# Two cached attention blocks on one core: three of the sixteen output-weight loads as sixteen transfers of 8 partitions each

## The chip, the cores and the metric

The kernel runs on one core of a Trainium2 chip. A core has five engines that run side by side: TensorE (PE; its weight loads are listed apart as PEld), VectorE (DVE), ScalarE (ACT), GpSimd (POOL) and SyncE (SP). Each has its own list of instructions and waits for the others by semaphores. Data comes from device memory into SBUF, which has 128 partitions, by DMA: an instruction on an engine's queue hands a transfer to the core's 16 DMA engines, which raise a semaphore when their share has landed. The metric is the time of one execution on the device in microseconds (us), lower being better.

## The reference, cut to what matters

Two independent blocks, A and B, with the same shapes; each is a decode step of attention over a key and value cache, followed by an output projection.

```python
def block(x, k_cache, v_cache, wq, wo):      # x [8, 1, 1024]; caches [8, 32, 4096, 128]; wq [1024, 4096]; wo [4096, 1024]
    q = (x @ wq).reshape(8, 1, 32, 128).transpose(0, 2, 1, 3)
    scores = jnp.einsum("bhqd,bhkd->bhqk", q, k_cache) * (128 ** -0.5)
    p = softmax(scores, axis=-1)
    o = jnp.einsum("bhqk,bhkd->bhqd", p, v_cache)
    return o.transpose(0, 2, 1, 3).reshape(8, 1, 4096) @ wo
out = concatenate([block(A), block(B)], axis=-1)
```

Everything is bfloat16. The four caches hold 256 MB each, and each is read once.

## The kernel before

**Steps.** The work is cut into 128 steps. A step is one batch row and one group of four heads: `gi` (0 to 15) counts cache and head group, and eight batch rows make up a group. One step needs 4 MB of keys and 4 MB of values. In SBUF a 4 MB load is 128 partitions by 32 KB: partition `h * 32 + p` holds 128 consecutive positions of head `h`.

**The loop.** Line 381 runs over `n`. In round `n` the keys of step `n` are loaded (`load_k`, line 217), multiplied by the query on DVE in two halves (`multiply`, line 263), summed over the head dimension by PE with the identity matrix (`add_up`, line 275) and by DVE (`reduce`, line 283). Step `m = n - 1` goes through its softmax on DVE and ACT, its values are loaded (`load_v`, line 224) and PE multiplies them with the probabilities (`pv`, line 321). Two rounds behind, PE and DVE gather the heads' outputs (`gather`, `heads`). Three rounds behind, after the last batch row of a group, `project` (line 347) multiplies the group's outputs with that group's 512 rows of the output weights and adds to the accumulator `acc`.

**Buffers and queues.** Keys and values have two buffers each (`NB = 2`), and so have the output weights (`wob`, one MB a buffer, chosen by `gi % 2`). Loads of keys, values and weights are all issued on SP's queue, in the order of the program: in round `n` first the keys of `n`, then, once in eight rounds (`m % 8 == 4`), the output weights of the group, then the values of `m`. SP holds an issue back until the buffer is free: a key load waits for DVE's last multiplication on that buffer, a value load for PE's `pv`. The two `x` loads and three of the four output stores are issued on ACT's queue; the last store is on SP's. These six transfers have 8 partitions each.

**The output-weight load.** `load_wo` (line 235) is one DMA per group. Its source is 512 rows of `wo`, its target 128 partitions by four pieces of 2 KB. It marks the buffer's name `wo0` or `wo1` as written, and `project` reads that name. The names are the planner's: `P.add` and `dma` record which operation reads and writes which name, `finish` turns that into semaphore waits in front of an instruction, and each DMA name has a semaphore of its own that counts to 16 per transfer. The weights of group `gi` are issued in the fifth round of the group and used five rounds later; for the first group that is 93.1 us and 231.3 us.

Of the kernel before, what the change touches and what calls it, by code (L numbers as in the profile page):

```python
# [94 lines left out]
def _build(nc, caches, out):  # L95
    x0, k0, v0, wq0, wo0 = caches[0]
    B, Sq, D = x0.shape
# [15 lines left out]
    assert Sq == 1 and Dh == 128 and Sk == 4096 and D == 1024 and H % HP == 0 and B == 8  # L113
    assert RS * H * Dh == T * Dh and R == NB * RS
    scale = float(Dh) ** -0.5

    es = ExitStack()
    with es:
        block = es.enter_context(nc.Block())

        def sb(name, shape, dt):
            return es.enter_context(nc.sbuf_tensor(name, shape, dt))

        def ps(name, shape):
            return es.enter_context(nc.psum_tensor(name, shape, FP32))
# [10 lines left out]
        wob = sb("wob", [128, 2, HP, D], BF16)  # L136
# [10 lines left out]
        on = sb("on", [128, 2, HP, B], BF16)  # L147
# [4 lines left out]
        acc = ps("acc", [128, 512])  # L152
# [4 lines left out]
        P = Program()  # L157

        def dma(eng, dst, src, writes, sem, reads=()):
            return P.add(eng, lambda e: e.dma_start(dst, src), reads=reads, writes=writes, dma=sem)  # L160
# [26 lines left out]
        def load_wq(which, c, s):  # L187
            i = slot(which)
            w = bufs[which][:, i, :].rearrange("p (r n) -> p r n", r=RS)
            src = caches[c][3].rearrange("(p r) n -> p r n", r=R)[:, s * RS:(s + 1) * RS, :]  # L190
            dma("sp", w, src, [f"{which}{i}"], f"{which}{i}")
            return f"{which}{i}", w
# [42 lines left out]
        def load_wo(gi):  # L235
            c, g = divmod(gi, NG)
            i = gi % 2
            src = caches[c][4][g * HP * Dh:(g + 1) * HP * Dh, :].rearrange("(h p) n -> p h n", p=Dh)
            dma("sp", wob[:, i], src, [f"wo{i}"], f"wo{i}")

        def make_qbc(n):
            gi, b0 = divmod(n, B)
# [104 lines left out]
        def project(gi):  # L347
            c, g = divmod(gi, NG)
            i = gi % 2

            def emit(e):
                last = None
                for hh in range(HP):
                    for half in range(2):
                        last = e.matmul(acc[32 * half:32 * half + B, :], on[:, i, hh, :], wob[:, i, hh, half * 512:(half + 1) * 512],  # L355
                                        start=(g == 0 and hh == 0), stop=(g == NG - 1 and hh == HP - 1),
                                        tile_position=(0, 32 * half))
                return last
            P.add("pe", emit, reads=[f"on{i}b{b}" for b in range(B)] + [f"wo{i}"], banks=["acc"])
            if g == NG - 1:  # L360
                for half, eng in ((0, "dve"), (1, "act")):
                    dst, src = orow[32 * half:32 * half + B, c, :], acc[32 * half:32 * half + B, :]
                    if eng == "dve":
                        P.add(eng, lambda e, dst=dst, src=src: e.tensor_copy(dst, src), writes=[f"orow{c}{half}"], banks=["acc"])
                    else:
                        P.add(eng, lambda e, dst=dst, src=src: e.activation(dst, src, ACTF.Copy), writes=[f"orow{c}{half}"], banks=["acc"])
                for half in (1, 0):
                    q = "sp" if c == NC - 1 and half == 0 else "act"
                    dma(q, out[:, 0, c * D + half * 512:c * D + (half + 1) * 512], orow[32 * half:32 * half + B, c, :],
                        [f"out{c}{half}"], "out", reads=[f"orow{c}{half}"])  # L370

        NS = NC * NG * B
        kslot, vslot = {}, {}
        first = [(s,) + load_wq("v", 0, s) for s in range(R // RS)]
        for c in range(NC):
            make_xT(c)
# [4 lines left out]
        for n in range(NS + 3):  # L381
# [3 lines left out]
            if 0 <= m < NS:  # L385
                last = m == NS - 1
                if m % B == 4 and m // B < NC * NG - 1:
                    load_wo(m // B)
                load_v(m, 4 if last else 1)
                if last:  # L390
                    load_wo(m // B)
# [12 lines left out]
            if n - 3 >= 0 and (n - 3) % B == B - 1:  # L404
                project((n - 3) // B)
# [58 lines left out]
def bass_concat_heads__mha_block_cached__mha_block_cached__decode_kernel(  # L464
    nc, A_x, A_k_cache, A_v_cache, A_wq, A_wo, B_x, B_k_cache, B_v_cache, B_wq, B_wo, out,
):
    caches = [(A_x, A_k_cache, A_v_cache, A_wq, A_wo), (B_x, B_k_cache, B_v_cache, B_wq, B_wo)]
    _build(nc, caches, out)
# [28 lines left out]
```

## Time and profile before

| what | value |
|---|---|
| median of 3 runs | 2599.2 us (2596.18 to 2600.48) |
| the profiled execution's own time | 2599.03 us |
| its span (first to last instruction) | 2597.2 us |
| around the span (own time less span) | 1.8 us |
| bytes read from device memory | 1107.33 MB, 426 GB/s over the span |
| PE busy | 1589.6 us (61%) |
| DVE busy | 1421.9 us (55%) |
| ACT busy | 391.0 us (15%) |
| output-weight loads | 16, 1024 KB each, 30.8 us from issue to landing |
| `project` on PE (line 355) | 128 matmuls, 16.6 us busy |

The profile is of one execution. "Busy" is the time in which an engine executed instructions, and engines overlap, so shares don't add up to one. For DMA the page has the mean busy share of the 16 DMA engines in 40 slices of the span, the packets of each queue, and the median time from the issue of a transfer to its landing; that time includes the wait behind transfers that were issued earlier. The chain of work that ended last is followed back from the last instruction, at each step to whatever released it. Besides the page, the trace holds a record for each DMA packet (start, duration, bytes, queue) and for each increment of a DMA semaphore.

### The profile page before, as it was taken

The numbers are of one execution on the slowest core, as the hardware profiler recorded it, in microseconds if no ns is written. First come the engines' busy times: TensorE is split into PE (matmuls) and PEld (weight loads), VectorE is DVE, ScalarE is ACT, GpSimd is POOL, SyncE is SP. The second block draws the span as 40 slices with busy tenths as digits, with TensorE's granted clock in tenths as the row PEclk, the third lists the DMA queues.
The fourth block names the chain that finished last, engine by engine and source line by source line (L and its number), as shares of the span: only waits on it lengthen the run. The fifth ranks groups of instructions, "written<-read, shape, count | busy, mean of one in ns | idle before, by whom it ended". The sixth has DMA issues, their size and how long they took to land.

```text
span 2597.2 us, 24223 instructions
## 1 busy us (share of the span) xinstructions
PE 1589.6 (61%) x10640; PEld 725.0 (28%) x10640; DVE 1421.9 (55%) x1291; ACT 391.0 (15%) x1187; POOL 1.6 (0%) x11
## 2 busy tenths in 40 slices
PE   4666566556655665666566556655666566566656
PEld 2222223222322322222223222322322232222223
DVE  3655565555535555655556555555655565565554
ACT  0111111111101111111111111111111111111111
POOL 0000000000000000000000000000000000000000
PEclk9788778877777878778778777887778778777877
DMA  9999999999999999999999999999999999999997
GB/s 420 427 433 430 429 431 429 431 432 428 431 428 432 431 428 433 429 430 432 428 432 428 432 430 428 432 429 428 432 431 429 431 431 429 430 432 430 429 432 315
DMA packets 46521, 1108.92 MB, mean 427 GB/s; under 512 B 4512, under 2 KB 4544, under 8 KB 12752
## 3 DMA queue, kind: packets, MB, share of 16 engines
q1 hardware_dynamic: 46336, 1107.32, 99.5%
q8 instruction: 83, 1.36, 0.2%
q14 instruction: 22, 0.18, 0.0%
q10 hardware_dynamic: 80, 0.06, 0.0%
HBM read 1107.33 MB, written 0.03 MB: 426 GB/s over the span
## 4 chain that ended last, share of the span: by engine, by line
DMA 73%; DVE 25%; PE 1%; issue 0%; ACT 0%; SPq 0%; DVEq 0%
DMA kbuf<-in_B_k_cache_dram 36%; DMA kbuf<-in_A_k_cache_dram 35%; DVE prod L263 22%; DVE score L283 1%; DMA kbuf<-in_B_wq_dram 1%; PE red L275 1%; DVE rmax L288 1%; DVE tmax L289 1%; DVE nmax L291 0%; DVE bias L293 0%; PE oacc L321 0%; PE qps L209 0%; PE sps L336 0%; ACT prob L297 0%; PE acc L355 0%
## 5 line engine op out<-in xcount | busy, mean ns | idle before, releaser
L275 PE MATMUL red<-prod,ident 128*128 128x512 bf16 x4096 | 1200.5, 459 | 976.3 <-DVE prod L263 976.3
L263 DVE TENSOR_TENSOR prod<-kbuf,qbc 128x8192 bf16<-128x8192 bf16 x256 | 1131.5, 4420 | 1035.6 <-DMA kbuf<-in_A_k_cache_dram 520.9
L275 PEld LDWEIGHTS red<-prod,ident 128*128 128x128 bf16 x4096 | 458.6, 117 | 1658.1 <-DVE prod L263 1028.7
L297 ACT ACTIVATE prob<-score,bias 32x128 bf16<-32x128 f32 x512 | 295.3, 577 | 1108.9 <-DVE bias L293 1098.0
L321 PE MATMUL oacc<-vbuf,prob 128*16 128x512 bf16 x4096 | 245.0, 381 | 0.0
L327 ACT ACTIVATE osb<-oacc 128x512 f32<-128x512 f32 x128 | 76.4, 597 | 1060.0 <-PE oacc L321 1060.0
L283 DVE TENSOR_REDUCE score<-red 128x64 f32<-128x512 f32 x256 | 175.6, 686 | 28.4 <-PE red L275 27.2
L336 PEld LDWEIGHTS sps<-sel,osb 128*128 128x128 f32 x1024 | 134.3, 191 | 20.8 <-issue 1.4
L321 PEld LDWEIGHTS oacc<-vbuf,prob 128*16 128x16 bf16 x4096 | 91.1, 89 | 143.4 <-issue 55.5
L297 ACT ACTIVATION_READ_ACCUMULATOR prob<-score,bias 32x1 f32 x512 | 128.3, 251 | 0.0
L336 PE MATMUL sps<-sel,osb 128*128 128x4 f32 x1024 | 121.9, 242 | 1.6 <-ACT osb L327 1.6
L304 PE MATMUL sps<-rsum,ones 128*128 128x4 f32 x256 | 47.2, 255 | 1.7 <-ACT prob L297 1.7
L344 DVE TENSOR_TENSOR on<-sps,rl 128x4 bf16<-128x4 f32 x128 | 22.3, 174 | 46.7 <-PE sps L304 40.6
L304 PEld LDWEIGHTS sps<-rsum,ones 128*128 128x128 f32 x256 | 39.0, 192 | 8.8 <-issue 6.5
L288 DVE TENSOR_REDUCE rmax<-score 128x1 f32<-128x128 f32 x128 | 36.6, 286 | 4.5
L289 DVE STREAM_TRANSPOSE tmax<-rmax 128x32 f32<-128x32 f32 x128 | 27.0, 211 | 4.4
L291 DVE TENSOR_REDUCE nmax<-tmax 128x1 f32<-128x32 f32 x128 | 23.8, 186 | 4.4
L256 ACT ACTIVATE qbc<-bps 128x512 bf16<-128x512 f32 x32 | 18.9, 592 | 25.6 <-PE bps L251 25.6
L309 DVE RECIPROCAL rl<-sps 128x4 f32<-128x4 f32 x128 | 22.1, 173 | 0.0
L293 DVE TENSOR_SCALAR bias<-nmax 128x1 f32<-128x1 f32 x128 | 19.7, 154 | 4.4
L215 DVE CAST qT<-qps 128x256 bf16<-128x256 f32 x2 | 0.9, 426 | 29.8 <-PE qps L209 29.8
L355 PE MATMUL acc<-wob,on 128*8 128x512 bf16 x128 | 16.6, 381 | 0.3 <-DVE on L344 0.3
(25 smaller groups left out, 66.0 us busy)
## 6 DMA issues: line engine op xcount, KB each, us to landing
kbuf<-in_A_k_cache_dram SPq DMA_DIRECT2D x64, 4096.0 KB, 28.5
vbuf<-in_A_v_cache_dram SPq DMA_DIRECT2D x64, 4096.0 KB, 32.7
kbuf<-in_B_k_cache_dram SPq DMA_DIRECT2D x64, 4096.0 KB, 28.5
vbuf<-in_B_v_cache_dram SPq DMA_DIRECT2D x63, 4096.0 KB, 32.5
vbuf<-in_A_wq_dram SPq DMA_DIRECT2D x2, 4096.0 KB, 17.3
wob<-in_A_wo_dram SPq DMA_DIRECT2D x8, 1024.0 KB, 30.8
kbuf<-in_B_wq_dram SPq DMA_DIRECT2D x2, 4096.0 KB, 29.1
wob<-in_B_wo_dram SPq DMA_DIRECT2D x8, 1024.0 KB, 30.8
```

The costliest lines, as they stand in the source:

```text
L263: P.add("dve", lambda e: e.tensor_tensor(pv, kv, qbc[:, qi, n % QT, :].unsqueeze(1).to_broadcast([128, CT, Dh]), ALU.mult), reads=[f"k{ki} ...
L275: last = e.matmul(rv, ident[:], pj[:, :, j, :], start=(j == 0), stop=(j == NJ - 1))
L283: P.add("dve", lambda e: e.tensor_reduce(dst, rv, AX.X, ALU.add), writes=[f"score{n % 2}c{ch}"], banks=[f"red{i}"])
L288: P.add("dve", lambda e: e.tensor_reduce(rmax[:, i:i + 1], score[:, i, :], AX.X, ALU.max), reads=sc, writes=[f"rmax{i}"])
L289: P.add("dve", lambda e: e.transpose(tmax[:, i, :], rmax[:, i:i + 1].to_broadcast([128, SEG])), reads=[f"rmax{i}"], writes=[f"tmax{i}"])
L291: P.add("dve", lambda e: e.tensor_reduce(nmax[:, i:i + 1], tmax[:, i, :], AX.X, ALU.max), reads=[f"tmax{i}"], writes=[f"nmax{i}"])
L297: P.add("act", lambda e, pr=pr, hh=hh: e.activation(prob[pr, i, :, hh], score[pr, i, :], ACTF.Exp, bias=bias[pr, i:i + 1], scale=scale, ac ...
L304: P.add("pe", lambda e: e.matmul(sps[:, i * HP:(i + 1) * HP], ones[:], rsum[:, i, :], start=True, stop=True), reads=[f"rsum{i}h{h}" for h ...
L321: last = e.matmul(oacc[i][32 * q:32 * q + TB * HP, :], prob[:, i, j * TB:(j + 1) * TB, :].rearrange("p t h -> p (t h)"), vbuf[:, vi, j * 5 ...
L327: P.add("act", lambda e: e.activation(osb[:, i, :], oacc[i][:], ACTF.Copy), writes=[f"osb{i}"], banks=[f"oacc{i}"])
L336: last = e.matmul(sps[:, o:o + HP], osb[:, i, t * Dh:(t + 1) * Dh], sel[:, t, :], start=(t == 0), stop=(t == TB - 1))
L344: P.add("dve", lambda e: e.tensor_tensor(on[:, gi % 2, :, b], sps[:, o:o + HP], rl[:, i, :], ALU.mult), reads=[f"rl{i}"], writes=[f"on{gi ...
```

## The change

Groups 2, 7 and 12 (two of cache A, one of cache B) load their output weights with sixteen DMAs in place of one. Each moves 8 partitions by four pieces of 2 KB, 64 KB in all, from the same rows of `wo` to the same place in `wob`, on the same queue and at the same place in the program. The first keeps the buffer's name `wo0` or `wo1`; the other fifteen have names and semaphores of their own (`wo0p1` to `wo0p15`, `wo1p1` to `wo1p15`). `project` now reads the names in `wparts[gi]`: sixteen for those three groups, one for the others.

```diff
+    EIGHTS = (2, 7, 12)
...
             src = caches[c][4][g * HP * Dh:(g + 1) * HP * Dh, :].rearrange("(h p) n -> p h n", p=Dh)
-            dma("sp", wob[:, i], src, [f"wo{i}"], f"wo{i}")
+            if gi in EIGHTS:
+                names = [f"wo{i}"] + [f"wo{i}p{q}" for q in range(1, 16)]
+                for q in range(16):
+                    r = slice(8 * q, 8 * q + 8)
+                    dma("sp", wob[r, i], src[r], [names[q]], names[q])
+                wparts[gi] = names
+            else:
+                dma("sp", wob[:, i], src, [f"wo{i}"], f"wo{i}")
+                wparts[gi] = [f"wo{i}"]
...
-            P.add("pe", emit, reads=[f"on{i}b{b}" for b in range(B)] + [f"wo{i}"], banks=["acc"])
+            P.add("pe", emit, reads=[f"on{i}b{b}" for b in range(B)] + wparts[gi], banks=["acc"])
...
-        kslot, vslot = {}, {}
+        kslot, vslot, wparts = {}, {}, {}
```

## The prediction

> **What bounds the kernel now.** I read the page first: DMA by slices, the queues, the chain that ended last, and the issues.
>
> ```profile
> span 2597.2 us, 24223 instructions
> ...
> DMA  9999999999999999999999999999999999999997
> ...
> DMA packets 46521, 1108.92 MB, mean 427 GB/s; under 512 B 4512, under 2 KB 4544, under 8 KB 12752
> ...
> q8 instruction: 83, 1.36, 0.2%
> ...
> q10 hardware_dynamic: 80, 0.06, 0.0%
> ...
> DMA 73%; DVE 25%; PE 1%; issue 0%; ACT 0%; SPq 0%; DVEq 0%
> ...
> kbuf<-in_A_k_cache_dram SPq DMA_DIRECT2D x64, 4096.0 KB, 28.5
> vbuf<-in_A_v_cache_dram SPq DMA_DIRECT2D x64, 4096.0 KB, 32.7
> ...
> wob<-in_A_wo_dram SPq DMA_DIRECT2D x8, 1024.0 KB, 30.8
> ```
>
> The 16 DMA engines are busy from end to end. By the semaphore records a 4 MB load lands 9.71 us after the one before it, a 1 MB weight load 2.53 to 2.70 us (median 2.66) after its predecessor. A key load lands 28.5 us after its issue though it needs 9.71, so 18.8 us of work lie ahead of it: the queue never runs dry. The 25% of DVE in the chain is the freeing of buffers, which this backlog covers. So the end is set by the sum of transfers, 260 x 9.71 + 16 x 2.66 = 2567 us, plus what delays the slowest DMA engine; all has landed at 2589.1, and a tail of 8 us follows.
>
> **Which DMA engine is the slowest.** A load has landed when its last engine is done, and engines don't wait for each other. I looked at the DMA view in short windows: around the first weight load, and three around the last one. In these windows only a weight load has packets of 2 KB, 512 of them, so "under 8 KB" less "under 2 KB" counts its packets.
>
> ```profile
> DMA packets 586, 2.41 MB, mean 401 GB/s; under 512 B 32, under 2 KB 32, under 8 KB 544
> ...
> DMA packets 418, 1.80 MB, mean 361 GB/s; under 512 B 32, under 2 KB 32, under 8 KB 261
> ...
> DMA packets 172, 1.10 MB, mean 221 GB/s; under 512 B 17, under 2 KB 17, under 8 KB 44
> ...
> DMA packets 287, 0.66 MB, mean 131 GB/s; under 512 B 16, under 2 KB 16, under 8 KB 272
> ```
>
> In 118 to 124 us all 512 pass. At the end 229 pass in 2574 to 2579, 27 in the next 5 us, 256 in 2584 to 2589: half of the engines are some 9 us ahead. The 16 semaphore records of each load show how that grows: eight engines stay within 2 us of the last one throughout, six run ahead (3 us at 440, 9 at 1250, 14 at 2050, 16 at 2400 us), two lie between. The late eight are held back in turn: in some 30 us one of them loses about 1.5 us, each time beside an instruction-fetch packet (the 83 of q8, about 1.05 us each).
>
> **How many engines a piece uses.** The semaphore writes are the packets under 512 B. 279 transfers of 128 partitions with 16 each make 4464; 4512 leaves 48, which is 8 for each of the six transfers of 8 partitions. So such a transfer runs on eight engines, and q10's 80 packets agree: 5 x (8 + 8). Which eight: around 1372 to 1377 us two stores, from partitions 0-7 and 32-39, go out amid the loads. Following each engine's packets end to start, both ran on the same eight: six ahead (by 9.6, 9.5, 9.3, 8.1, 5.9 and 4.6 us) and two of the late ones (1.9 and 1.6 us before the last).
>
> [...]
>
> **The change, part by part.**
>
> *Bytes per engine.* A split sends 1 MB through eight engines. Those have 64 packets of 2 KB in place of 32, 2.66 us more; the other eight have none, 2.66 us less. Fifteen more semaphore writes per engine at 9 ns (their packet records) are 0.14 us. So +2.8 us on each of the eight per split, +8.4 for three.
>
> *What that does to the end.* The six that lead have 10.5 to 16 us in hand at the end, or 7.4 for the nearest, and don't matter much: 8.4 leaves the nearest 1.0 behind the old end. The two late ones had 1.7 us in hand at the last landing (the engine that came last had just been hit by a fetch). They end 8.4 - 1.7 = 6.7 us later. The late ones outside the eight gain 8 us, which is worth nothing once the two are last. Bounds: 8.4 if the fetches fall on them last, 4.9 if they have 3.5 in hand.
>
> *Issue on SP.* The timeline of SP around the load of group 2:
>
> ```profile
> 410.54 0.33 SPq L160 DMA_DIRECT2D kbuf<-in_A_k_cache_dram  x1
> ...
> 410.91 0.43 SPq L160 DMA_DIRECT2D wob<-in_A_wo_dram  x1
> ...
> 416.97 0.33 SPq L160 DMA_DIRECT2D vbuf<-in_A_v_cache_dram  x1
> ...
> 429.98 0.33 SPq L160 DMA_DIRECT2D kbuf<-in_A_k_cache_dram  x1
> ```
>
> Sixteen issues at 0.33 to 0.43 us plus 0.04 between are 5.9 to 7.5 us; SP is done by 416.8 to 418.4, so the value load behind them goes out at most 1.5 us late. It would have stood behind 32.7 - 9.7 = 23 us of queued work: cost 0. Without that cover it would be 1.5 x 3 = 4.5 us. The next key issue, at 429.98, is untouched.
>
> *Waits.* `project` waits for sixteen semaphores in place of one, 45 more waits on PE. Behind them stands the next `add_up`, for which PE idles anyway:
>
> ```profile
> PE red L275 <- DVE prod L263: 976.3, 129, 11.0
> ```
>
> Some 7.6 us a round. The weights are used 138 us after their issue (93.1 to 231.3 for group 0) and land after 31, so none of the waits is held. Cost 0; uncovered, at 0.1 us a wait (an estimate, over twice the 0.04 us between two issues on SP), 4.5.
>
> *Conflicts between the eight.* All eight now write neighbouring partitions. The trace of before has only the `x` load for that: at 6.1 us eight packets of 2 KB went to partitions 0-7, up to four at once, each in 84 ns, as a weight packet among loads (81 to 88). That speaks for nothing. The last stores speak for something: eight packets of 1 KB read from neighbouring partitions took 46 to 47 ns each when spread out (1373 us), but 49 to 107 when started together (2595.7 us). I take 0, by the `x` packets, which are writes of the same size; the upper bound is twice the duration for all 64 packets, +5.3 us a split, +16 in all.
>
> [...]
>
> **Sum.** Against the profiled execution's own 2599.03: +8.4 - 1.7 = +6.7, or 2605.7; the median of the runs, 2599.2, lies 0.2 above it, so I say 2606.
>
> **Rivals.**
>
> *Conflicts on shared partitions* (slower still). For: the last stores. Against: the `x` packets, and that the six leading engines are 3 to 14 us ahead at the three splits, so mainly the two late ones can meet. Price: up to 16 on top, 2622; half of it, 2614.
>
> *The load is levelled* (not slower). If the eight on SP's queue hold only engines that lead by more than 8.4 us, the late ones lose 2.66 a split and the others stay hidden: 2599 - 8 = 2591. It decides when no late engine is among the eight. For: the growing lead. Against: the two late ones at 1372 us. In a milder form, where the two among the eight are hit by one or two fetches fewer, at 1.5 each, it comes out near 2603.
>
> *The pieces spread over all engines.* If each transfer takes a different eight, every engine has its old bytes and 24 semaphore writes more (0.2 us): 2599.3. Against: the same eight for both stores.
>
> **How the numbers follow.** Doubling on a fixed eight, 2603 to 2609: 52%. Conflicts, 2609 to 2624: 24%. Spread, or the milder levelling, 2597 to 2603: 17%. Full levelling, about 2591: 7%. A measurement can tell about 0.2%, 5.2 us, from no change: slower begins at 2604.4. Of the first case three quarters lie above it, with the second that makes 63% for slower; 30% within; 7% faster. Leaving out the levelling and the ends of the rest, the range is 2599 to 2623; the likeliest case alone has 2603 to 2609.
>
> **What would show it.** Right: packets under 512 B rise by 3 x (16 x 8 - 16) = 336 to 4848; the records of the weights landing at about 442, 1258 and 2053 us show the same eight engines in all pieces; after each split those are some 5.5 us later against the others than before it; loads still land 9.71 apart between splits; the last landing is at 2596. Wrong: 16 or rotating engines (the spread), 2 KB packets well over 84 ns (conflicts), a gap in the DMA slices after 418 us (the issue on SP), or PE idle at line 355 with a DMA as releaser.

## The result, and the profile after

The changed kernel takes 2623.78 us (median of 4 runs, 2619.28 to 2625.11) against 2599.59 us for the kernel before, run beside it: 24.2 us more, a ratio of 1.0092 with a 95% interval of 1.008 to 1.0104. The prediction was 2606, with a range of 2599 to 2623. The profiled execution took 2619.28 us, the fastest of the four.

The page's line of GB/s in 40 slices, first for the kernel before:

```profile
GB/s 420 427 433 430 429 431 429 431 432 428 431 428 432 431 428 433 429 430 432 428 432 428 432 430 428 432 429 428 432 431 429 431 431 429 430 432 430 429 432 315
```

and the lines of the changed kernel's page:

```profile
span 2617.4 us, 24292 instructions
...
GB/s 416 432 431 430 429 430 394 430 432 429 430 427 432 431 428 431 430 430 430 374 431 428 431 431 430 430 429 432 429 430 432 360 431 431 430 431 429 431 432 343
DMA packets 46857, 1108.92 MB, mean 424 GB/s; under 512 B 4848, under 2 KB 4880, under 8 KB 13088
...
DMA 73%; DVE 25%; PE 1%; issue 0%; ACT 0%; SPq 0%; DVEq 0%
```

Bytes are the same, and the chain of waits has the same shares. The time went in three places: of the 40 slices, three that had 428 to 431 GB/s now have 394, 374 and 360, and they are the slices of the three split loads (65 us each, so the 7th, 20th and 32nd hold 430, 1260 and 2060 us). Packets under 512 B, the semaphore writes, are 336 more, as eight engines for each piece make it.

The issues on SP around the load of group 2 (start, duration, what; sixteen issues merged into one row):

```profile
410.50 0.33 SPq L161 DMA_DIRECT2D kbuf<-in_A_k_cache_dram  x1
410.87 24.33 SPq L161 DMA_DIRECT2D wob<-in_A_wo_dram  x16
435.30 0.36 SPq L161 DMA_DIRECT2D vbuf<-in_A_v_cache_dram  x1
435.70 0.43 SPq L161 DMA_DIRECT2D kbuf<-in_A_k_cache_dram  x1
```

Where the prediction had SP done after 5.9 to 7.5 us, it stands 24.3 us in the sixteen issues. The single records show eleven issues of 0.3 to 0.5 us, and then four of 2.4 to 8.5 us: SP stands in these.

The DMA view of 1240 to 1285 us, around the split load of group 7: first the kernel before, then the change (busy tenths and GB/s in slices of 1.1 us).

```profile
DMA  9899799999989989999989999999999998999999
...
DMA packets 1155, 19.26 MB, mean 428 GB/s; under 512 B 86, under 2 KB 86, under 8 KB 598
```

```profile
DMA  9989999999989745533949979499699999999988
GB/s 408 437 379 408 408 437 466 466 437 408 408 346 266 175 120 157 189 126 118 413 124 377 289 188 417 118 350 337 268 408 466 466 437 466 408 451 466 437 350 379
DMA packets 1135, 15.49 MB, mean 344 GB/s; under 512 B 181, under 2 KB 181, under 8 KB 693
```

Two things show. From about 1254 to 1261 us the busy share falls to 0.3 to 0.7: engines are idle, because the value load is issued only when SP is free again, at 1260.65 us. From 1261 to 1273 us the engines are mostly busy, and still only 118 to 417 GB/s move: packets take longer. The packet records say how much. This is worked out from them for the three split loads in each kernel, beside the same loads of the kernel before; a packet of 32 KB belongs to the key and value loads around them.

```
                 packets of 2 KB, median ns    longest packet of 32 KB, ns
kernel before        85    86    86             1252   1593   1705
the change          148   114   113             2674   2264   2285
```

An undisturbed packet of 32 KB takes 1215 ns. In the change, 78, 110 and 128 of them around the three loads were stretched by over 30 ns. The semaphore records give the bill of each split: the key load before it and the value load behind it (with the weights between) land 9.71 and 12.37 us apart when undisturbed, and 11.42 + 17.73, 12.59 + 17.92 and 12.40 + 17.37 us here, so 7.1, 8.4 and 7.7 us more. Their sum is 23.2, and the last key load is late by nearly that, 23.0: DVE starts on it at 2589.9 us instead of 2566.9.

So there were three candidates: the doubled bytes on eight engines (the prediction's own term), SP's long stand (Q in the expectations below), and the slower packets (N, if engines that write neighbouring partitions slow each other; S, if each small transfer costs a fixed time).

### The profile page after: what moved, and what is told of

It is laid out like the page before. It is cut to its first block, busy times and chain, and to the rows that moved or that the text cites. A ratio compares the mean times of both kernels' runs of the same rounds, so it can differ in the third digit from the quotient of the medians.

```text
span 2617.4 us, 24292 instructions
## 1 busy us (share of the span) xinstructions
PE 1579.9 (60%) x10640; PEld 721.7 (28%) x10640; DVE 1420.2 (54%) x1291; ACT 390.8 (15%) x1187; POOL 1.6 (0%) x11
## 2 busy tenths in 40 slices
DMA packets 46857, 1108.92 MB, mean 424 GB/s; under 512 B 4848, under 2 KB 4880, under 8 KB 13088
## 4 chain that ended last, share of the span: by engine, by line
DMA 73%; DVE 25%; PE 1%; issue 0%; ACT 0%; SPq 0%; DVEq 0%
DMA kbuf<-in_B_k_cache_dram 36%; DMA kbuf<-in_A_k_cache_dram 36%; DVE prod L272 21%; DVE score L292 1%; DMA kbuf<-in_B_wq_dram 1%; DVE rmax L297 1%; DVE tmax L298 1%; PE red L284 1%; DVE nmax L300 0%; DVE bias L302 0%; PE oacc L330 0%; PE qps L210 0%; ACT prob L306 0%; PE sps L345 0%; ACT osb L336 0%
```

## The experiments

All have the change's three groups unless it is said otherwise. Medians are of the runs beside runs of the kernel before on the same chip; the kernel before took 2598.47 us beside e1 to e4, 2599.88 beside e5 to e8 and 2599.18 beside e9.

**e1: pieces of every fourth partition.** The eight partitions of a piece are 4 apart in place of neighbours; everything else stays.

```diff
-                    r = slice(8 * q, 8 * q + 8)
+                    a = 32 * (q // 4) + q % 4
+                    r = slice(a, a + 29, 4)
```

> The same sixteen pieces of 8 partitions, bytes, engines and semaphores for the three groups, but each piece takes every fourth partition of a block of 32 (source rows likewise) in place of eight neighbours. N (engines that write neighbouring partitions slow each other; this took most of the 24 us): only the doubling on eight engines is left, 2603 to 2609, packets of 2 KB back at a median of 84 to 90 ns in all three splits. Q (SP stands 24 to 29 us in sixteen issues, so loads start late): SP stalls as before, 2619 to 2625. S (small transfers cost a fixed time on the engines): 2619 to 2625.

Measured: 2615.67 us, ratio 1.007 (1.0055 to 1.0085). Between the two expectations, and the packets say why. Around the first split load those that started before 438 us took 84 to 89 ns, all of them; those from 439 us on took 128 to 193, in the median 168. The first eight pieces go to partitions 0 to 63, the last eight to 64 to 127. Around this load 60 packets of 32 KB took over 1300 ns, half of these over 2170. Both sorts took about twice their time: 168 ns against 84, and over 2170 against 1215. In the other two splits the median over all 512 packets of 2 KB was 84 and 85 ns, as N expected, and only 65 and 105 of them took over 140. But the slow ones come at the end: the last 64 had a median of 174 ns, and these belong to the engines that finish last. Theory N, neighbours, was too narrow; I put O in its place: an engine is slowed where it writes partitions that another engine is writing, and in a full load each engine has partitions of its own. A full load has 128 packets of 32 KB, one for each partition, and at 1215 ns eight of them take 9.72 us, the 9.71 us between two landings: eight to an engine. Which partitions are whose no record shows. O takes partitions 0 to 63 for the eight engines' own, by the two halves of the first split, 84 to 89 ns and 168.

**e2: the same targets, other source rows.**

```diff
+                    a = 32 * (q // 4) + q % 4
                     r = slice(8 * q, 8 * q + 8)
-                    dma("sp", wob[r, i], src[r], [names[q]], names[q])
+                    dma("sp", wob[r, i], src[a:a + 29:4], [names[q]], names[q])
```

> Targets as in the change (eight neighbouring partitions a piece), source rows taken as in e1 (every fourth of 32), so the weights of these three groups stand in other rows and the output changes. N with the conflict in SBUF: as the change, 2617 to 2626, packets of 2 KB at 110 to 150 ns. If the conflict is at the source, in neighbouring rows of device memory: as e1 by that reading, 2603 to 2609. Q and S: 2619 to 2625.

Measured: 2624.68 us, ratio 1.0101 (1.0086 to 1.0117), packets of 2 KB at 146, 118 and 118 ns in the median: as the change. The rows in device memory have no part in it; the targets in SBUF have.

**e3: four pieces in each of four rounds.**

```diff
-                for q in range(16):
+                for q in range(4 * part, 4 * part + 4):
...
+                elif m % B > 4 and m // B in EIGHTS:
+                    load_wo(m // B, m % B - 4)
```

> The pieces of the change, four in each of four rounds instead of sixteen in one, so that SP never has more than four small issues in a row. Q: no issue on SP takes over 1 us and the cost falls to the doubling, 2603 to 2609. N: SP is free too, but neighbours are still written together, 2612 to 2625, packets of 2 KB over 100 ns. S: 2619 to 2625.

Measured: 2636.61 us, ratio 1.0151 (1.0136 to 1.0166), 13 us worse than the change. SP was free, as the timeline of its queue shows:

```profile
410.92 1.39 SPq L161 DMA_DIRECT2D wob<-in_A_wo_dram  x4
416.15 0.36 SPq L161 DMA_DIRECT2D vbuf<-in_A_v_cache_dram  x1
...
430.36 1.70 SPq L161 DMA_DIRECT2D wob<-in_A_wo_dram  x4
435.94 0.35 SPq L161 DMA_DIRECT2D vbuf<-in_A_v_cache_dram  x1
```

With no stand the cost is not less but more, so Q doesn't explain the loss; no theory had foreseen 2636. Stretched packets of 32 KB were 275, 514 and 552 around the three groups, some four times those of the change. That four separate groups of pieces meet four times with loads at full speed, where the change meets them once and partly with idle engines, is my reading and was not tested further.

**e4: eight pieces of 16 partitions.** All 16 engines take part (4848 packets under 512 B, so 16 semaphore writes a piece), and no engine has more bytes than before.

```diff
-                for q in range(16):
-                    r = slice(8 * q, 8 * q + 8)
+                for q in range(8):
+                    r = slice(16 * q, 16 * q + 16)
```

> Eight pieces of 16 partitions for the same three groups: all 16 engines take part (16 semaphore writes a piece), so no engine has more bytes than before; eight issues, fewer than the eleven after which SP stood. N: every piece still brings neighbours together, 2603 to 2618, packets of 2 KB over 100 ns in part. Q: no stall, 2598 to 2602. S (a fixed time per small transfer, now half as many): 2605 to 2612. If only doubling mattered: 2598 to 2602.

Measured: 2618.58 us, ratio 1.0076 (1.0059 to 1.0093); packets of 2 KB at 148, 145 and 146 ns, of 32 KB up to 2799. Just above N's range, and well over Q's 2602 and S's 2612: without any doubling and with 0.43 us for each issue (no stand), slow packets alone cost some 20 us. By O, the spread of the same bytes over partitions that aren't the engine's own is enough.

**e5 and e6: only the first or only the last eight of e1's pieces.** The same bytes and number of transfers; only the half of the partitions differs, and with it the rows of the weights.

```diff
-                for q in range(16):
-                    r = slice(8 * q, 8 * q + 8)
+                for q in range(8):
+                    a = 0 + 32 * (q // 4) + q % 4      # e6: 64 + ...
+                    r = slice(a, a + 29, 4)
```

> Only the first eight of e1's pieces: partitions 0 to 63 of the three groups' weights, 512 KB on the eight engines, so as many bytes for each of them as before the change. Partitions 64 to 127 of these groups are not loaded, and the output changes. O (an engine is slowed where it writes partitions that are another engine's in a full load; the first half is these engines' own): packets of 2 KB stay at 84 to 88 ns, no packet of 32 KB over 2000 ns, time 2594 to 2601. F (a fixed cost for each small transfer): half of the cost of e1, 2604 to 2609.

> Only the last eight of e1's pieces: partitions 64 to 127, the same eight engines, bytes and number of transfers as e5. Partitions 0 to 63 of these groups are not loaded, and the output changes. O: these partitions are the other eight engines' own, so packets of 2 KB at a median of 150 to 180 ns, packets of 32 KB up to 2300 ns and more, time 2603 to 2613. F: the same as e5, within 2 us.

Measured: e5 2598.73 us, ratio 0.9996 (0.9986 to 1.0006); e6 2614.72 us, ratio 1.0062 (1.0047 to 1.0077). The DMA view of 1250 to 1268 us, first e5, then e6:

```profile
DMA packets 414, 7.86 MB, mean 437 GB/s; under 512 B 61, under 2 KB 61, under 8 KB 181
...
q1 hardware_dynamic: 413, 7.85, 101.8%
```

```profile
DMA packets 430, 4.29 MB, mean 238 GB/s; under 512 B 74, under 2 KB 74, under 8 KB 314
...
q1 hardware_dynamic: 430, 4.29, 97.4%
```

In both the engines are busy throughout (102 and 97% of 16 engines), but in e6 they move little over half as much. Packets of 2 KB had medians of 84 to 85 ns in e5 and 169 to 171 in e6, the longest of 32 KB 1764 and 2506. 16 us lie between partitions 0 to 63 and 64 to 127, by O between "own" and "another engine's". The rows read differ too, but e9 below reads the rows of e6 into partitions 0 to 63, and its packets of 2 KB stay at 84 ns. F, a fixed cost of small transfers (S in e1 to e4), falls: e5's twenty-four transfers of 64 KB, with the eight engines' bytes as before the change, cost nothing that can be measured.

**e7: eight transfers over all 128 partitions, by columns.**

```diff
-                    r = slice(8 * q, 8 * q + 8)
-                    dma("sp", wob[r, i], src[r], [names[q]], names[q])
+                    hh, r = q // 2, slice(512 * (q % 2), 512 * (q % 2) + 512)
+                    dma("sp", wob[:, i, hh, r], src[:, hh, r], [names[q]], names[q])
```

> Eight transfers for the same three groups, each over all 128 partitions and a quarter of a half (one head, 512 of 1024 columns, rows of 1 KB): split, but every engine stays on its own partitions and has its old bytes. O: no stretched packets, 2598 to 2603. F: as e4, 2610 to 2620. On SP: if it stands after a number of transfers (eleven small ones in the change), no issue is over 1 us; if after a number of packets waiting on an engine (9 each here, 5 in the change), it stands after six or seven.

Measured: 2599.97 us, ratio 0.9999 (0.9989 to 1.0008), with no packet of 32 KB much stretched, but for eight at 1253 us, where loads start again on engines that had run dry (up to 2229 ns). And yet SP stood:

```profile
410.78 17.78 SPq L161 DMA_DIRECT2D wob<-in_A_wo_dram  x8
429.04 6.85 SPq L161 DMA_DIRECT2D vbuf<-in_A_v_cache_dram  x1
435.95 0.42 SPq L161 DMA_DIRECT2D kbuf<-in_A_k_cache_dram  x1
```

Six issues took 0.43 us each and the seventh 6.44. Six by 9 packets on each engine are 54; in the change eleven by 5 are 55, and in e1 and e9 twelve by 5 are 60 (all at group 2). So SP stood once 54 to 60 small packets per engine were queued behind the loads, and not after a fixed number of transfers: it was six, eleven and twelve. And a stand of 25 us in all, as long as the change's, costs nothing here: Q falls by itself.

**e8: the change for group 7 alone** (`EIGHTS = (7,)`).

> The change for group 7 alone. Any theory in which a split costs its own time: a third of the 24 us, 2605 to 2609. If the cost of a split hangs on the ones before it (the late engines fall behind once and later splits are hidden, or grow): under 2603 or over 2611.

Measured: 2607.3 us, ratio 1.0033 (1.0021 to 1.0045), so 7.4 us: about a third of the change's 24.2. This split pays for itself.

**e9: the doubling alone.** Sixteen pieces, all to partitions 0 to 63, half of them into a spare buffer.

```diff
+        wsc = sb("wsc", [128, HP, D], BF16)
...
-                    r = slice(8 * q, 8 * q + 8)
-                    dma("sp", wob[r, i], src[r], [names[q]], names[q])
+                    a = 32 * (q // 4 % 2) + q % 4
+                    b = a + 64 * (q // 8)
+                    dst = (wob[:, i] if q < 8 else wsc[:])[a:a + 29:4]
+                    dma("sp", dst, src[b:b + 29:4], [names[q]], names[q])
```

> Sixteen pieces for the three groups, all to partitions 0 to 63: the eight pieces of e5 into the weights' buffer, and eight more (the rows that belong to partitions 64 to 127) to the same partitions of a spare buffer that nobody reads. Partitions 64 to 127 of these weights are not loaded, and the output changes. Bytes per engine, number of transfers and issues on SP are those of the change; only the partitions are the eight engines' own. Doubling alone, as the prediction priced it (+2.8 us a split on two late engines with some 1.7 in hand): packets of 2 KB at 84 to 88 ns, SP standing in its issues as in the change, 2603 to 2609. If the standing of SP costs: 2610 or more. If doubling costs nothing on the whole: 2597 to 2601.

Measured: 2607.03 us, ratio 1.0031 (1.0019 to 1.0043), 7.9 us more than the 2599.18 beside it; packets of 2 KB at 84 ns in the median in all three splits. Of the packets of 32 KB 8, 13 and 14 took over 1300 ns around the splits (in the change 74, 106 and 117), nearly all where the value load starts again on engines that had run dry. SP stood as in the change:

```profile
410.91 5.90 SPq L162 DMA_DIRECT2D wob<-in_A_wo_dram  x8
416.85 19.90 SPq L162 DMA_DIRECT2D wsc<-in_A_wo_dram  x8
436.85 0.38 SPq L162 DMA_DIRECT2D vbuf<-in_A_v_cache_dram  x1
```

So 7.9 of the change's 24.2 us are the doubling on eight engines. By O the remaining 16.3, by subtraction, fall to engines writing into each other's partitions, if the two add up; e6 and e4, which have no doubling, lost 14.8 and 20.1 us that way. No version tried beats the kernel before; e5 and e7 equal it, and e5 leaves half of three loads out.

## Why the prediction went wrong, by its own steps

**The bound.** Right. The slowest of the DMA engines sets the end, and what a split adds to it arrives in full: 23.2 us by the landings, 23.0 at the last key load. The tail behind it was some 3 us shorter in this execution (2617.4 - 2589.9 = 27.5, before 2597.2 - 2566.9 = 30.3), which is why the profiled run shows only 20 us.

**Eight engines, the same eight.** Right: 4848 semaphore writes as foretold, and e5 against e6 speaks for a fixed eight: 2 KB took 84 to 85 ns into partitions 0 to 63 and 169 to 171 into 64 to 127. A rotating choice would have made the two halves alike.

**The doubling.** Right in mechanism and size: +6.7 foretold, +7.9 measured alone in e9 (interval 4.9 to 11). After the change's third split two engines run last (2.3 us apart at the last load), the next 5.6 ahead, which fits the two late ones among the eight.

**Issue on SP, cost 0.** The cost was right, the duration not: 24 to 29 us in place of 5.9 to 7.5, since SP stood from the twelfth issue on, up to 12.4 us in one, which no row of before showed. What hid it was the backlog named there, and beyond it the lead of the engines that ran dry; e7 stood as long and lost nothing, and e9 stood as long and lost no more than the doubling was priced at, give or take its interval. In the change the value load behind the pieces is issued at 435.3, 1260.65 and 2065.9 us, each time before the last engine has landed its key load (440.7, 1264.5 and 2068.6), so the engine that sets the end never waits for SP.

**Waits of `project`, cost 0.** Right. The waits of the changed kernel name no DMA for that line:

```profile
PE acc L364 <- DVE on L353: 0.3, 1, 0.3
```

**Conflicts between the eight: here it failed.** The step took 0, "by the `x` packets, which are writes of the same size". Sixteen kilobytes at the start of the kernel were no test: packets of 2 KB at 84 ns showed a short burst of one packet for each engine, while a split has 64 in a row. And they were one `x` load of two: the packet records have eight more packets of 2 KB at 1.70 to 2.05 us, the other `x` load, which took 81 to 459 ns, the four that started together 108 to 459. Whether shared partitions or the start of the kernel slowed those is not shown, but "the `x` packets" did not speak for 0 with one voice. The runs put 16.3 us in the place of 0, and the sign that the prediction named for it, packets of 2 KB well over 84 ns, is there (113 to 148). The upper bound, "+5.3 us a split, +16 in all", has about that size, but for a wrong reason. It doubled the packets of the eight engines alone, and the two late ones only where they meet. What e1 and e6 show is that key and value packets are slowed too, where the eight write into partitions that O takes for the other engines': in e6 those over 1300 ns had medians of 2265, 2120 and 1794 ns in the three splits, in place of 1215. And in the change the key load, which is queued ahead of the pieces, lands 1.7 to 2.9 us late. The rival "conflicts on shared partitions" said 2614 to 2622, its band of 2609 to 2624 holds the 2623.78, and it should have had the first place: the last stores (49 to 107 ns together, 46 alone) were the better row.

## What to carry to other kernels

A transfer over few partitions was slow twice here: one of 8 partitions ran on only eight engines (7.9 us for the three groups, e9), and these wrote where, by O, other engines were at work, which slowed loads that have nothing to do with it (packets of 32 KB up to 2506 ns in place of 1215, 14.8 us in e6). When a load has to be split, split it along the rows, so that each part still covers all 128 partitions: e7 did that at no cost (2599.97 us against 2599.88). In a kernel bound by DMA, look at the sixteen landings of each load rather than at the mean busy share: in the kernel before six engines were 8.5 to 9.3 us ahead of the last at 1255 us. Here a stand of 25 us on the issuing queue was free (e7), while what the splits put on the late engines arrived in full (23.2 us by the landings, 23.0 at the last key load).

## What the runs showed of the hardware that was not expected

- The eight engines of the pieces got about half their rate into partitions 64 to 127, and so did others beside them: 2 KB in some 170 ns in place of 84 (e1, e6), 32 KB in 1794 to 2265 in the median of the slowed ones in place of 1215 (e6). That it is two engines writing into the same partitions is O's reading. The DMA busy share didn't show it (97% in e6, 102% in e5); GB/s did (238 against 437).
- The issuing queue stood when 54 to 60 small packets per engine were queued behind the loads (six transfers of 9 in e7, eleven of 5 in the change, twelve of 5 in e9), and a single issue then lasted up to 12.4 us (the change, group 12).
- Undisturbed 4 MB loads landed every 9.71 us throughout, and still the 16 engines behind them drifted apart by up to 16.9 us over the kernel before: eight of them lost some 1.5 us in turn beside the 83 instruction fetches (a fetch of 1.07 us, then a packet of 32 KB at 1.68 to 1.76 us in place of 1.215, in six of them from 635 to 772 us).
